# Channel attention and a GELU feed-forward on one core: the second layer of each pair's first chunk by Strassen's scheme over halves, the first layer's products on two PSUM banks

## The chip, the core and the metric

The kernel runs on one core of a Trainium2 chip. The engines that matter here are PE (TensorE: matrix products, each with a load of its stationary operand, a weight load, shown as PEld), DVE (VectorE: elementwise work and sums), ACT (ScalarE: activations and copies) and SP (SyncE, which only issues the DMAs). PE writes its results to PSUM, which has eight banks of 128 x 512 fp32 words; DVE and ACT read them there. The metric is the device time of one execution in microseconds; less is better.

## The reference

```python
def _attn_ref(q, k, v, tau):                      # B, N, C = 4, 6080, 256
    qn = q / (np.linalg.norm(q, axis=1, keepdims=True) + 1e-06)
    kn = k / (np.linalg.norm(k, axis=1, keepdims=True) + 1e-06)
    s = kn.transpose(0, 2, 1) @ qn / tau
    s = s - s.max(-1, keepdims=True)
    a = np.exp(s)
    a /= a.sum(-1, keepdims=True) + 1e-09
    return (v @ a).astype(np.float32)

def _moe_ref(x, w_in, w_out):                     # d_model 256, d_ff 2048
    h = x @ w_in
    g = 0.5 * h * (1.0 + erf(h * inv_sqrt2))
    return (g @ w_out).astype(np.float32)
```

The output is `_moe_ref` of the attention's output, reshaped to 24320 tokens. The attention is over channels, so `a` is only 256 x 256 per batch.

## The kernel before

The 256 x 256 matrix `a` of a batch is folded into the input weights (`w_group`: `e` times `w_in`), so that the rest of a batch is two layers: the hidden values from v (first layer, with a GELU), and the output from the hidden values (second layer, with `w_out`). Every fp32 operand is split into a high part in the reduced fp32 format of PE and a low part that is the difference, and each product is made by three matmuls: high x high, high x low, low x high.

Tokens are in columns. A batch has six *pairs* (`PAIRS`): pair p holds two *chunks* j = 0, 1 of n = 512 tokens each, 480 in the last pair. The hidden dimension of 2048 is cut into eight *units* u of 256, each of two row blocks i = 0, 1. One (b, p, u) is a *step*; there are 4 x 6 x 8 = 192.

- `first_products` makes the four hidden blocks (i, j) of a step by Winograd's form of Strassen's scheme over rows and chunks: seven products in `ORDER`, each of three matmuls of n columns (L459 to L461, tile `ph`), 21 in all. The pool `ps_h` gives it PSUM banks out of four: `one` collects products 0, 2, 4 and 6, `two` products 1 and 5, `three` product 3. ACT copies intermediate sums out (`kept`, L479: p1, p5, u2), DVE adds them to later ones (`added`, L484: h).
- `gelu` (L467 to L469) runs the activation twice on ACT, once into the reduced format (gh) and once in fp32 (g), and DVE subtracts for the low part gl. `plain_products` does the same without Strassen for pair (0,0), before the sums of the weights exist.
- `second_products` multiplies the blocks of the step before with `w_out` (L554 to L556, tile `po`): for each chunk j, row block i and output half c three matmuls, 24 a step. Four banks of `ps_o` collect the eight units of a pair; after the last, ACT and DVE copy them to `osb` (L560, L562) and SP stores them (L567).
- PE alternates: the main loop draws one group of `second_products` after each product of the first layer.

`extras` adds the work that isn't part of the step: `load_wo` (L267, the split `w_out` of a later step, kept in DRAM, three buffers), the loads and splits of v of the next pair (`load_v`, `v_sums`, `v_split` L446, L447), and for the next batch the loads of q and k (L128), their split (`split_qk`, L181 and L182, both on DVE), the score *bursts* (`burst`, L191 and L193, 8 matmuls for each half m, added to `sacc` by DVE, L201), the norms (`norm_part`, L208 load and L209 square on ACT), the softmax in stages, and `w_group`.

The program is written in the order of the loops; a planner then orders each engine's queue by that order and by its own estimate of when an instruction can run, and assigns the buffers of each pool as they come free.

## Time and profile before

| | |
|---|---|
| median of 3 runs | 2198.34 us (2194.01 to 2200.15) |
| profiled execution | 2194.5 us, span of its instructions 2192.7 us |
| busy share of the span | PE 99%, weight loads 82%, DVE 63%, ACT 65% |
| DMA, mean | 122 GB/s, 35.7% of 16 engines |
| weight loads and matmuls | 9664 of each |

A row of a group reads: line, engine, operation, output <- inputs, sizes, count | busy us, mean ns of one | idle time of the engine before them, and what ended it. A row of the timeline reads: start, duration, engine, line, operation, with the idle time before it in brackets. A row of the waits reads: total us, times, longest.

### The profile page before, as it was taken

How to read it: one execution, taken by the hardware profiler on the slowest of the kernel's cores; microseconds unless marked ns; L12 is line 12 of the kernel's file. 1: busy time of each engine (PE TensorE's matmuls, PEld its weight loads, DVE VectorE, ACT ScalarE, POOL GpSimd, SP SyncE). 2: the span in 40 equal slices, each digit the busy share in tenths (PEclk: the TensorE clock that was granted, in tenths of full speed). 3: DMA queues.
4: the chain of work that ended last, by engine and by line, in shares of the span. 5: the costliest groups of instructions: out<-in, count | busy, mean ns of one | idle time of the engine just before them, and what ended most of it. 6: DMA issues, size and time to landing. Idle time of an engine off the chain costs nothing.

```text
span 2192.7 us, 26257 instructions
## 1 busy us (share of the span) xinstructions
PE 2180.0 (99%) x9664; PEld 1792.8 (82%) x9664; DVE 1391.5 (63%) x2186; ACT 1432.3 (65%) x2602; POOL 1.3 (0%) x8
## 2 busy tenths in 40 slices
PE   9999999999999999999999999999999999999999
PEld 7787778888888888888888888888888888888888
DVE  6995757666586675765667657667466555555554
ACT  5678886658866565565766656656576666666665
POOL 0000000000000000000000000000000000000000
PEclk9999999999999999999999999999999999999999
DMA  9467774323752332322224323232122121121121
GB/s 382 171 220 253 243 246 135 105 87 107 254 176 96 97 113 80 121 97 69 97 97 143 119 74 125 78 107 93 49 106 96 58 95 68 68 95 68 68 77 48
DMA packets 77056, 267.52 MB, mean 122 GB/s; under 512 B 7680, under 2 KB 9728, under 8 KB 74880
## 3 DMA queue, kind: packets, MB, share of 16 engines
q1 hardware_dynamic: 76928, 265.84, 35.7%
q8 instruction: 76, 1.25, 0.2%
q14 instruction: 52, 0.43, 0.1%
HBM read 232.52 MB, written 33.29 MB: 121 GB/s over the span
## 4 chain that ended last, share of the span: by engine, by line
PE 89%; ACT 5%; DMA 5%; DVE 1%; issue 0%; SPq 0%; ACTq 0%; DVEq 0%
PE po L556 15%; PE po L554 14%; PE po L555 14%; PE ph L461 12%; PE ph L460 12%; PE ph L459 12%; DMA kqc<-kqt 4%; PE ph L191 3%; ACT kqc L209 2%; PE ph L149 2%; PE ph L531 2%; PE ph L193 1%; ACT gh L467 1%; ACT g L468 1%; PE ph L390 1%; PE ph L388 1%
## 5 line engine op out<-in xcount | busy, mean ns | idle before, releaser
L469 DVE TENSOR_TENSOR gl<-g,gh 128x512 fp32r<-128x512 f32 (+1 forms) x768 | 522.3, 682 | 157.7 <-ACT g L468 155.7
L556 PE MATMUL po<-gh,wo 128*128 128x512 f32 (+1 forms) x1536 | 602.4, 394 | 0.0
L554 PE MATMUL po<-gh,wo 128*128 128x512 f32 (+1 forms) x1536 | 599.0, 390 | 0.0
L555 PE MATMUL po<-gl,wo 128*128 128x512 f32 (+1 forms) x1536 | 596.0, 388 | 1.1 <-DVE gl L469 1.1
L484 DVE TENSOR_TENSOR h<-ph,p 128x512 f32<-128x512 f32 (+1 forms) x368 | 251.6, 684 | 518.8 <-PE ph L461 411.8
L467 ACT ACTIVATE gh<-h 128x512 fp32r<-128x512 f32 (+1 forms) x552 | 345.8, 626 | 283.1 <-DVE h L484 280.8
L459 PE MATMUL ph<-vh,wh 128*128 128x512 f32 (+1 forms) x1288 | 502.8, 391 | 3.0 <-ACT p L479 1.6
L461 PE MATMUL ph<-vh,wl 128*128 128x512 f32 (+1 forms) x1288 | 503.7, 391 | 0.0
L460 PE MATMUL ph<-vl,wh 128*128 128x512 f32 (+1 forms) x1288 | 502.7, 390 | 0.0
L479 ACT COPY p<-ph 128x512 f32<-128x512 f32 (+1 forms) x368 | 213.2, 584 | 245.0 <-PE ph L461 244.7
L555 PEld LDWEIGHTS po<-gl,wo 128*128 128x128 f32 x1536 | 288.3, 188 | 65.6 <-DVE gl L469 2.0
L554 PEld LDWEIGHTS po<-gh,wo 128*128 128x128 f32 x1536 | 288.4, 188 | 62.4 <-ACT wo L246 1.0
L556 PEld LDWEIGHTS po<-gh,wo 128*128 128x128 f32 x1536 | 288.2, 188 | 61.8 <-DVE wo L248 0.5
L468 ACT ACTIVATE g<-h 128x512 f32<-128x512 f32 (+1 forms) x552 | 337.7, 612 | 0.0
L459 PEld LDWEIGHTS ph<-vh,wh 128*128 128x128 f32 x1288 | 242.0, 188 | 58.8 <-ACT p L479 5.0
L460 PEld LDWEIGHTS ph<-vl,wh 128*128 128x128 f32 x1288 | 242.1, 188 | 54.0
L461 PEld LDWEIGHTS ph<-vh,wl 128*128 128x128 f32 x1288 | 241.9, 188 | 49.1
L479 ACT COPY u<-ph 128x512 f32<-128x512 f32 (+1 forms) x184 | 107.1, 582 | 112.9 <-PE ph L461 112.9
L467 ACT ACTIVATE gh<-ph 128x512 fp32r<-128x512 f32 (+1 forms) x216 | 125.1, 580 | 13.0 <-PE po L556 8.3
L484 DVE TENSOR_TENSOR h<-ph,u 128x512 f32<-128x512 f32 (+1 forms) x184 | 125.7, 683 | 3.4
L468 ACT ACTIVATE g<-ph 128x512 f32<-128x512 f32 (+1 forms) x216 | 126.5, 587 | 0.3 <-DVE gl L469 0.3
L191 PE MATMUL ph<-hl 128*128 128x512 f32 x272 | 96.0, 392 | 0.0
(138 smaller groups left out, 1423.2 us busy)
## 6 DMA issues: line engine op xcount, KB each, us to landing
wo<-keep_out SPq DMA_DIRECT2D x184, 512.0 KB, 3.2
raw<-qk SPq DMA_DIRECT2D x95, 512.0 KB, 4.6
kqc<-kqt SPq DMA_DIRECT2D x72, 512.0 KB, 4.5
v_raw<-vt SPq DMA_DIRECT2D x20, 1024.0 KB, 5.0
out<-osb SPq DMA_DIRECT2D x40, 512.0 KB, 3.1
win<-keep_in SPq DMA_DIRECT2D x12, 1024.0 KB, 5.0
raw<-w_in SPq DMA_DIRECT2D x8, 512.0 KB, 7.2
raw<-w_out SPq DMA_DIRECT2D x8, 512.0 KB, 4.4
```

The lines of the kernel that those rows point to most:

```text
L191: nc.tensor.matmul(s, hl[:, 0, j, 0, cs], hl[:, :, j, 1], start=(i == 0), stop=False, skip_group_check=True)
L459: nc.tensor.matmul(ps[:, :n], wh, hi[:, :n], start=start, stop=False, skip_group_check=True)
L460: nc.tensor.matmul(ps[:, :n], wh, lo[:, :n], start=False, stop=False, skip_group_check=True)
L461: nc.tensor.matmul(ps[:, :n], wl, hi[:, :n], start=False, stop=stop, skip_group_check=True)
L467: nc.scalar.activation(out=gh[:, :n], in_=src, func=AF.Gelu)
L468: nc.scalar.activation(out=g[:, :n], in_=src, func=AF.Gelu)
L469: nc.vector.tensor_tensor(out=gl[:, :n], in0=g[:, :n], in1=f32(gh[:, :n]), op=ALU.subtract)
L479: nc.scalar.copy(out=t[:, :n], in_=ps[:, :n])
L484: nc.vector.tensor_tensor(out=h[:, :n], in0=ps[:, :n], in1=t[:, :n], op=ALU.add)
L554: nc.tensor.matmul(o, wo[:, 0, i, cs], gh[:, :n], start=first, stop=False)
L555: nc.tensor.matmul(o, wo[:, 0, i, cs], gl[:, :n], start=False, stop=False)
L556: nc.tensor.matmul(o, wo[:, 1, i, cs], gh[:, :n], start=False, stop=last)
```

## The change

Chunk 1 is computed as before. For chunk 0 the second layer is computed by Winograd's form of Strassen's scheme as well, over the two halves of the chunk's columns, the two row blocks of the unit and the two output halves: seven products of n/2 columns (`work` in `second_products`) in place of four of n. They need sums of the gelu values (`sums`: the activation once in fp32 into `x` by `whole`, three instructions of sums on DVE, the high parts copied by ACT, the low parts subtracted by DVE) and sums of `w_out` (`sum_wo`, made once in pair (0,1), kept in DRAM, loaded for each step by `load_ws`). The seven products go to halves of the banks c00, c01, p0 and p1, which collect over the units; `combine` and `merge` add them up at the end of a pair. It holds for the steps named by `strassen`.

With p0 and p1 in use, the first layer has two banks, h0 and h1 (`ring`, `bank`, `later`), and another `ORDER`. PE's instructions are pinned to the order of the program (`pe`, `mm`). The scores' and weights' high parts are made by ACT instead of DVE (`split_qk`, `w_both`), a step holds one burst or one part of a weight group in place of two, `wo` has two buffers instead of three, the norms' tiles share the ring `raw` (four buffers) and the windows of the input weights the ring `hl` (three).

```diff
-    ps_h = ctx.enter_context(tc.tile_pool(name="ps_h", bufs=4, space=bass.MemoryType.PSUM))
-    ps_o = ctx.enter_context(tc.tile_pool(name="ps_o", bufs=4, space=bass.MemoryType.PSUM))
+    ps = ctx.enter_context(tc.tile_pool(name="ps", bufs=1, space=bass.MemoryType.PSUM))
...
+    def psum(name):
+        return ps.tile([P, NT], F32, name=name)
+
+    ring = deque(("h0", "h1"))
+
     def bank():
-        return ps_h.tile([P, NT], F32, name="ph")
-
+        name = ring.popleft()
+        ring.append(name)
+        return psum(name)
+
+    def later(name):
+        ring.remove(name)
+        ring.append(name)
+
+    def pe(op, *args, **kw):
+        r = op(*args, **kw)
+        if "filled" in state:
+            tc.keep_in_program_order(r)
+        return r
+
+    def mm(*args, **kw):
+        return pe(nc.tensor.matmul, *args, **kw)
...
     def split_qk(b, js):
         raw = raws.pop((b, js))
-        hl = pqk.tile([P, 2, JS, 2, C], F32R, name="hl")
-        nc.vector.tensor_copy(out=hl[:, 0], in_=raw)
+        hl = pqk.tile([P, 2, JS, 2, C], F32R, name="hl", bufs=3)
+        nc.scalar.copy(out=hl[:, 0], in_=raw)
         nc.vector.tensor_tensor(out=hl[:, 1], in0=raw, in1=f32(hl[:, 0]), op=ALU.subtract)
...
     def new_wo(key):
-        wos[key] = pw.tile([P, 2, 2, C], F32R, name="wo", bufs=3)
+        wos[key] = pw.tile([P, 2, 2, C], F32R, name="wo", bufs=2)
...
+    keep_sum = [pdram.tile([P, 2, 4, P], F32, name=f"keep_sum{u}") for u in range(NU)]
+    wss = {}
+
+    def new_ws(key):
+        wss[key] = pw.tile([P, 2, 4, P], F32R, name="ws", bufs=2)
+
+    def load_ws(key):
+        new_ws(key)
+        nc.sync.dma_start(out=f32(wss[key]), in_=keep_sum[key[2]])
+
+    def sum_wo(u):
+
+        wo = wos[0, 1, u]
+        x = pg.tile([P, 2, NT], F32, name="x", bufs=1)
+        full = x[:, 0].rearrange("p (f c) -> p f c", f=2)
+        s1, s2, s3, s4 = (x[:, 1, i * P:(i + 1) * P] for i in range(4))
+        a11, a12, a21, a22 = (full[:, 1 - k, c * P:(c + 1) * P] for c in range(2) for k in range(2))
+        tt = nc.vector.tensor_tensor
+        tt(out=full, in0=f32(wo[:, 0]), in1=f32(wo[:, 1]), op=ALU.add)
+        tt(out=s1, in0=a21, in1=a22, op=ALU.add)
+        tt(out=s3, in0=a11, in1=a21, op=ALU.subtract)
+        tt(out=s2, in0=s1, in1=a11, op=ALU.subtract)
+        tt(out=s4, in0=a12, in1=s2, op=ALU.subtract)
+        new_ws((0, 1, u))
+        ws = wss.pop((0, 1, u))
+        hi, lo = (ws[:, i].rearrange("p s c -> p (s c)") for i in range(2))
+        nc.scalar.copy(out=hi, in_=x[:, 1])
+        tt(out=lo, in0=x[:, 1], in1=f32(hi), op=ALU.subtract)
+        nc.sync.dma_start(out=keep_sum[u], in_=f32(ws))
...
-    def w_group(b, g):
+    def w_part(b, g, m):
...
+        win = wins[b, g]
+        if m == 0:
+            wtmp[g] = pqk.tile([P, 8, 2, P], F32, name="hl", bufs=3)
+        tmp = wtmp[g]
+        cs = slice(m * P, (m + 1) * P)
+        pwt = bank()
+        for d in range(NCT):
+            mm(pwt, eh[:, d, cs], win[:, 0, d], start=(d == 0), stop=False)
+            mm(pwt, eh[:, d, cs], win[:, 1, d], start=False, stop=False)
+            mm(pwt, el[:, d, cs], win[:, 0, d], start=False, stop=(d == NCT - 1))
+        nc.scalar.activation(out=tmp[:, 2 * m:2 * m + 2], in_=pwt.rearrange("p (q r c) -> p r q c", q=2, r=2),
...
+            w_both(whs[g][:, to], wls[g][:, to], tmp[:, of])
...
-    ORDER = ((A11, B11), (S1, T1), (S2, T2), (A12, B21), (S3, T3), (S4, B22), (A22, T4))
+    ORDER = ((A11, B11), (S1, T1), (S2, T2), (S4, B22), (S3, T3), (A12, B21), (A22, T4))
+
+    def passes(o, wh, wl, hi, lo, start, stop):
+        mm(o, wh, hi, start=start, stop=False, skip_group_check=True)
+        mm(o, wh, lo, start=False, stop=False, skip_group_check=True)
+        mm(o, wl, hi, start=False, stop=stop, skip_group_check=True)
...
+    def strassen(b, p, u):
+        return p > 1 if b == 0 else (b, p, u) != (B - 1, NP - 1, NU - 1)
+
+    def gelu(src, n, i, j):
+        if j == 1:
+            gh = pg.tile([P, NT], F32R, name="gh", bufs=2)
+            gl = pg.tile([P, NT], F32R, name="gl", bufs=2)
+        else:
+            gh = pg.tile([P, 4, C] if i == 0 else [P, 3, C], F32R, name=f"gh{i}", bufs=1)
+            gl = pg.tile([P, 4, C] if i == 0 else [P, 3, C], F32R, name=f"gl{i}", bufs=1)
+            gh, gl = (t.rearrange("p k c -> p (k c)") for t in (gh, gl))
...
         return gh, gl
 
+    def whole(src, n, i):
+
+        if i == 1:
+            state["x"] = pg.tile([P, 8 * C], F32, name="x", bufs=1)
+        at = 0 if i == 1 else n
+        nc.scalar.activation(out=state["x"][:, at:at + n], in_=src, func=AF.Gelu)
+
+    def sums(n):
+
+        h = n // 2
+        x = state["x"]
+        b11, b22, b21 = (x[:, k * h:(k + 1) * h] for k in (1, 2, 3))
+        t3, t2, t4 = (x[:, k * h:(k + 1) * h] for k in (5, 6, 7))
+        tt = nc.vector.tensor_tensor
+        hb = pg.tile([P, 3 * C], F32R, name="gh1", bufs=1)
+        lb = pg.tile([P, 3 * C], F32R, name="gl1", bufs=1)
+        ht = pg.tile([P, 4 * C], F32R, name="gh0", bufs=1)
+        lt = pg.tile([P, 4 * C], F32R, name="gl0", bufs=1)
+        state["blocks"]["b"], state["blocks"]["t"] = (hb, lb), (ht, lt)
+        tt(out=x[:, 4 * h:6 * h].rearrange("p (k c) -> p k c", k=2),
+           in0=x[:, h:3 * h].rearrange("p (k c) -> p k c", k=2),
+           in1=x[:, 0:h].unsqueeze(1).broadcast_to([P, 2, h]), op=ALU.subtract)
+        nc.scalar.copy(out=hb[:, :3 * h], in_=x[:, h:4 * h])
+        yield
+        tt(out=t2, in0=t3, in1=b11, op=ALU.add)
+        tt(out=t4, in0=b21, in1=t2, op=ALU.subtract)
+        nc.scalar.copy(out=ht[:, :4 * h], in_=x[:, 4 * h:8 * h])
+        tt(out=lb[:, :3 * h], in0=x[:, h:4 * h], in1=f32(hb[:, :3 * h]), op=ALU.subtract)
+        tt(out=lt[:, :4 * h], in0=x[:, 4 * h:8 * h], in1=f32(ht[:, :4 * h]), op=ALU.subtract)
...
-            t = pg.tile([P, NT], F32, name=name, bufs=2 if name == "p1" else 1)
+            t = pg.tile([P, NT], F32, name=name, bufs=1)
...
+        def chunk0(src, i):
+            if strassen(b, p, u):
+                whole(src, n, i)
+            else:
+                out[i, 0] = gelu(src, n, i, 0)
+
+        name = ring[0]
         one = bank()
         do(0, one, True, False)
         p1 = kept(one, "p1")
@@ -498,18 +593,21 @@
         do(2, one, False, False)
         u2 = kept(one, "u2")
         yield
-        three = bank()
-        do(3, three, True, True)
-        out[1, 0] = gelu(added(three, p1), n)
+        do(3, two, False, True)
+        out[1, 1] = gelu(added(two, u2), n, 1, 1)
         yield
         do(4, one, False, False)
-        out[0, 1] = gelu(added(one, p5), n)
-        yield
-        do(5, two, False, True)
-        out[1, 1] = gelu(added(two, u2), n)
+        out[0, 1] = gelu(added(one, p5), n, 0, 1)
+        yield
+        do(5, two, True, True)
+        chunk0(added(two, p1), 1)
         yield
         do(6, one, False, True)
-        out[0, 0] = gelu(one[:, :n], n)
+        chunk0(one[:, :n], 0)
+        later(name)
+        if strassen(b, p, u):
+            state["sums"] = sums(n)
+            next(state["sums"])
...
     def second_products(b, p, u, blocks):
 
         t0, n = PAIRS[p]
+        h = n // 2
         wo = wos.pop((b, p, u))
-        for j in range(2):
+        mine = strassen(b, p, u)
+        if u == 0:
+            po.clear()
+            po["mixed"] = any(strassen(b, p, x) for x in range(NU))
+            po["plain"] = not all(strassen(b, p, x) for x in range(NU))
+
+        def acc(name):
+            first = name not in po
+            if first:
...
+        def group(i, j, c):
+            o, first = acc(f"c{j}{c}")
+            gh, gl = blocks[i, j]
+            passes(o[:, :n], *wpair(c, i), gh[:, :n], gl[:, :n], first, u == NU - 1 and i == 0)
...
+        for i in (1, 0):
+            for c in range(NCT):
+                group(i, 1, c)
+                if u == NU - 1 and i == 0:
+                    evict(1, c)
+                yield
+        if not mine:
             for i in (1, 0):
-                gh, gl = blocks[i, j]
...
+                    if u == NU - 1 and i == 0:
+                        if po["mixed"]:
+                            merge(b, p, c)
+                            if c == 1:
+                                store(0, po["y"])
                         else:
-                            nc.vector.tensor_copy(out=osb[:, 1, :n], in_=o)
-                            t = b * N + t0 + j * n
-                            dst = out[:, t:t + n].rearrange("(t p) n -> p t n", p=P)
-                            step = 1 if (b, p) == (B - 1, NP - 1) else NCT
-                            for h in range(0, NCT, step):
-                                nc.sync.dma_start(out=dst[:, h:h + step], in_=osb[:, h:h + step, :n])
+                            evict(0, c)
                     yield
+            return
+        ws = wss.pop((b, p, u))
+        (hb, lb), (ht, lt) = blocks["b"], blocks["t"]
+        last = not any(strassen(b, p, x) for x in range(u + 1, NU))
+        work = (("c00", 1, wpair(0, 0), hb, lb, 2), ("p0", 0, wpair(0, 1), hb, lb, 0),
+                ("c00", 0, (ws[:, 0, 3], ws[:, 1, 3]), hb, lb, 1), ("p1", 0, (ws[:, 0, 0], ws[:, 1, 0]), ht, lt, 0),
+                ("p1", 1, (ws[:, 0, 2], ws[:, 1, 2]), ht, lt, 1), ("p0", 1, (ws[:, 0, 1], ws[:, 1, 1]), ht, lt, 2),
+                ("c01", 1, wpair(1, 0), ht, lt, 3))
+        for name, half, w, hi, lo, k in work:
+            o, first = acc(name)
+            passes(o[:, half * h:(half + 1) * h], *w, hi[:, k * h:(k + 1) * h], lo[:, k * h:(k + 1) * h], first, last)
+            if name == "c01":
+                if last:
+                    combine(b, p)
+                    if u == NU - 1:
+                        merge(b, p, 0)
+                        merge(b, p, 1)
+                        store(0, po["y"])
+            yield
...
+    def combine(b, p):
+
+        n = PAIRS[p][1]
+        h = n // 2
+        y = po["y"] = pg.tile([P, NCT, NT], F32, name="osb", bufs=2)
+        p0, p1 = po["p0"], po["p1"]
+        tt = nc.vector.tensor_tensor
+        nc.scalar.copy(out=y[:, 0, h:n], in_=p0[:, 0:h])
+        tt(out=y[:, 0, 0:h], in0=p0[:, h:n], in1=y[:, 0, h:n], op=ALU.add)
+        tt(out=y[:, 1, h:n], in0=p1[:, h:n], in1=y[:, 0, 0:h], op=ALU.add)
+        tt(out=y[:, 1, 0:h], in0=y[:, 1, h:n], in1=p1[:, 0:h], op=ALU.subtract)
+        tt(out=y[:, 0, 0:h], in0=y[:, 0, 0:h], in1=p1[:, 0:h], op=ALU.subtract)
+
+    def merge(b, p, c):
+
+        n = PAIRS[p][1]
+        lo = 0 if c == 0 or po["plain"] else n // 2
+        y = po["y"][:, c, lo:n]
+        nc.vector.tensor_tensor(out=y, in0=po[f"c0{c}"][:, lo:n], in1=y, op=ALU.add)
...
-    pg = ctx.enter_context(tc.tile_pool(name="pg", bufs=5))
+    pg = ctx.enter_context(tc.tile_pool(name="pg", bufs=1))
...
-    with tc.high_priority(), behind("fill"):
-        w_group(0, 0)
     for _ in fill:
         pass
+    ring.extend(("p0", "p1"))
+    with tc.high_priority(), behind("fill"):
+        for m in range(NCT):
+            w_part(0, 0, m)
...
+    def ahead(b, p, u):
+
+        def after(k):
+            i = (b * NP + p) * NU + u + k
+            return i // NU // NP, i // NU % NP, i % NU
+
+        nxt = after(2)
         if nxt[0] < B and nxt[:2] != (0, 0):
             load_wo(nxt)
+        nxt = after(1)
+        if nxt[0] < B and strassen(*nxt):
+            load_ws(nxt)
...
-        if b > 0 and w == 1:
-            w_group(b, NWG - 1)
+        if b > 0 and w == 0:
+            w_part(b, NWG - 1, 1)
...
+            if w in (at, at + 1):
+                burst(b + 1, k, w - at)
+            if w == at + 1:
                 for t in range(NB):
                     hls.pop((b + 1, k * NB + t))
+        for k in range(FILL // NB if b == 0 else 0, NQS // NB):
+            at = start + k * num // den
...
-        if w == 37:
-            state["stages"] = softmax(False, ps_h, "ph")
-        if w >= 37:
+        if w == 36:
+            state["stages"] = softmax(False)
+        if w >= 36:
             next(state["stages"], None)
-        if w in (40, 42, 44, 46):
-            load_win(b + 1, (w - 40) // 2)
-        if w in (42, 44, 46):
-            w_group(b + 1, (w - 42) // 2)
+        if w >= 41:
+            w_part(b + 1, (w - 41) // 2, (w - 41) % 2)
+        if w in (39, 41, 43, 45):
+            load_win(b + 1, (w - 39) // 2)
...
+    second, count = iter(()), 0
...
+        if (b, p) == (0, 1) and u == 0:
+            for name in ("p0", "p1"):
+                ring.remove(name)
         for i, _ in enumerate((plain_products if plain else first_products)(b, p, u)):
-            next(second, None)
+            for _ in range(1 if i < 4 or count < 11 else 2):
+                next(second, None)
...
+        if (b, p) == (0, 1):
+            sum_wo(u)
+        ahead(b, p, u)
         extras(b, p, u)
+        for _ in state.pop("sums", ()):
+            pass
+        count = 11 if strassen(b, p, u) else 8
         second = second_products(b, p, u, state.pop("blocks"))
```

More of the change, by code (lines that the diff above doesn't have):

```diff
@@ L314, in softmax @@
         yield
-        rq = pool.tile([P, NT], F32, name=name)
-        nc.tensor.matmul(rq[:, 0:C], ones, diag.rearrange("p h d -> p (h d)"), start=True, stop=True)
+        rq = psum("c10") if first else bank()
+        mm(rq[:, 0:C], ones, diag.rearrange("p h d -> p (h d)"), start=True, stop=True)
         for m in range(NCT):
@@ L331, in softmax @@
         yield
-        tp = pool.tile([P, NT], F32, name=name)
+        tp = psum("c11") if first else bank()
         tpv = tp.rearrange("p (d c) -> p d c", d=NCT)
```

125 lines of the change are left out of this document (52 added, 73 removed).

## The prediction

> **What bounds the kernel now.** I read the page's head, its 40 slices and its chain first, then TensorE's waits, then the busy time by stretches.
>
> ```profile
> span 2192.7 us, 26257 instructions
> PE 2180.0 (99%) x9664; PEld 1792.8 (82%) x9664; DVE 1391.5 (63%) x2186; ACT 1432.3 (65%) x2602; POOL 1.3 (0%) x8
> PEclk9999999999999999999999999999999999999999
> PE 89%; ACT 5%; DMA 5%; DVE 1%; issue 0%; SPq 0%; ACTq 0%; DVEq 0%
> ...
> PE ph L459 <- ACT p L479: 1.6, 2, 1.2
> PE ph L459 <- ACT u L479: 1.1, 2, 0.8
> PE po L555 <- DVE gl L469: 1.1, 2, 0.6
> ...
> 55.00:165.00 110.00, 108.77 (x467) 85.92 (x466) 106.89 (x211) 77.17 (x148) 0.00 (x0) 1.00 0.58 196
> 165.00:330.00 165.00, 163.16 (x714) 130.49 (x713) 101.41 (x155) 139.97 (x266) 0.00 (x0) 1.00 0.75 246
> 600.00:1100.00 500.00, 499.54 (x2228) 410.34 (x2227) 325.38 (x502) 313.31 (x567) 0.00 (x0) 1.00 0.32 108
> 1600.00:2190.00 590.00, 589.20 (x2602) 487.51 (x2600) 328.71 (x519) 380.76 (x693) 0.00 (x0) 1.00 0.22 77
> ```
>
> TensorE (PE) is busy for 99% of the span at full clock and hardly ever waits for another engine: behind the start, the waits above are its longest, 3.8 us together. The stretches (columns: length, then busy PE, weight load, DVE, ACT, POOL, clock, DMA share, GB/s) say the same of every stage. So time is what PE issues times the pitch of each instruction, and the change must be priced there first. VectorE (DVE) and ScalarE (ACT) come second: 65% busy in the third stretch, but 97% (DVE) in the first and 85% (ACT) in the second.
>
> A matmul's row says 0.39 us, but matmuls overlap; the pitch is the distance between starts:
>
> ```profile
> 1996.17 0.39 PE L461 MATMUL ph<-vh,wl 128*128 128x512 f32 x1
> ...
> 1996.65 0.69 DVE L484 TENSOR_TENSOR h<-ph,p 128x512 f32<-128x512 f32 x1 [4.08 <-PE ph L461]
> ...
> 2000.08 0.39 PE L460 MATMUL ph<-vl,wh 128*128 128x512 f32 x1
> 2000.31 0.39 PE L461 MATMUL ph<-vh,wl 128*128 128x512 f32 x1
> ...
> 2007.02 0.69 DVE L484 TENSOR_TENSOR h<-ph,p 128x512 f32<-128x512 f32 x1 [4.08 <-PE ph L461]
> ...
> 544.03 0.38 PE L461 MATMUL ph<-vh,wl 128*128 128x480 f32 x1
> 544.25 0.38 PE L554 MATMUL po<-gh,wo 128*128 128x480 f32 x1
> 544.47 0.38 PE L555 MATMUL po<-gl,wo 128*128 128x480 f32 x1
> ```
>
> A step (one unit u: 21 first-layer and 24 second-layer matmuls) takes 2007.02 - 1996.65 = 10.37 us, so 10.37/45 = 0.2305 us for 512 columns; 480 columns take 0.2175.
>
> **The change, part by part: the matmuls.** Per step 12 matmuls of chunk 0's second layer (four blocks of three passes) become 7 products x 3 passes = 21 matmuls of half the columns: 256, or 240 in the last pair. All hangs on the pitch of a narrow matmul that loads its own weights. The trace has one neighbour, the score bursts, which alternate 512 and 256 columns, and a floor, 16 matmuls of one column:
>
> ```profile
> 303.54 0.40 PE L191 MATMUL ph<-hl 128*128 128x512 f32 x1
> 303.78 0.28 PE L193 MATMUL ph<-hl 128*128 128x256 f32 x1
> 303.89 0.39 PE L191 MATMUL ph<-hl 128*128 128x512 f32 x1
> ...
> 303.78 0.19 PEld L191 LDWEIGHTS ph<-hl 128*128 128x128 f32 x1
> ...
> 50.30 1.84 PE L172 MATMUL po<-ones,acc 128*128 128x1 f32 x16
> ```
>
> The 256-column matmul starts at 303.78, the next one at 303.89, and the load for that next one also starts at 303.78. So 256 columns hide a whole weight load. Rounded starts give 0.11, half of 0.2305 is 0.115; I take 0.117, the burst's pair (0.35) less a wide one, rounded up. The floor is at most 1.84/16 = 0.115 us for a load with next to no columns: 256 columns lie just above it, and 240, by columns 0.109, may be held by it; I take 0.112 there.
>
> - 512-column step: 12 x 0.2305 - 21 x 0.117 = 2.766 - 2.457 = 0.309 us saved.
> - 480-column step: 12 x 0.2175 - 21 x 0.112 = 2.610 - 2.352 = 0.258 us.
>
> The predicate `strassen` holds in 32 steps of batch 0 (pairs 2 to 5) and in all 144 of batches 1 to 3 but the last: 175, of which 8 + 23 = 31 have n = 480. Saved: 144 x 0.309 + 31 x 0.258 = 44.5 + 8.0 = **52.5 us**. Bounds: with 0.115 and 0.109 it is 60; with 0.132 a matmul it is nothing.
>
> The Trainium skill speaks against this: "TensorE: Matmul & The Clock Gate", Part 3, "The mechanism", says that a weight load overlaps running matmuls only where the row groups differ, and these loads take all 128 rows. By it every one of the 9 added matmuls of a step would show its load. The trace disagrees (load and matmul both start at 303.78, the next matmul 0.11 us later). That rule is rival C below.
>
> **VectorE and ScalarE.** Rows for what is added and removed:
>
> ```profile
> L469 DVE TENSOR_TENSOR gl<-g,gh 128x512 fp32r<-128x512 f32 x640 | 438.7, 688 | 127.5 <-ACT g L468 125.9
> L405 DVE TENSOR_TENSOR wl<-hl,wh 128x1024 fp32r<-128x1024 f32 x12 | 14.7, 1225 | 0.3
> L405 DVE TENSOR_TENSOR wl<-hl,wh 128x768 fp32r<-128x768 f32 x12 | 11.4, 953 | 0.0
> L400 DVE TENSOR_TENSOR hl<-hl 128x256 f32<-128x256 f32 x12 | 5.1, 426 | 13.4 <-ACT hl L391 13.4
> L181 DVE CAST hl<-raw 128x1024 fp32r<-128x1024 f32 x68 | 46.3, 688 | 0.0
> L201 DVE TENSOR_TENSOR sacc<-ph,sacc 128x512 f32<-128x512 f32 x64 | 44.1, 690 | 12.9 <-PE ph L193 12.8
> ...
> L467 ACT ACTIVATE gh<-h 128x512 fp32r<-128x512 f32 x456 | 287.9, 631 | 243.8 <-DVE h L484 243.3
> L468 ACT ACTIVATE g<-ph 128x512 f32<-128x512 f32 x184 | 108.5, 591 | 0.3 <-DVE gl L469 0.3
> L479 ACT COPY p<-ph 128x512 f32<-128x512 f32 x304 | 177.8, 588 | 225.0 <-PE ph L461 225.0
> L350 ACT CAST wh<-hl 128x1024 fp32r<-128x1024 f32 x4 | 4.2, 1047 | 0.0
> ```
>
> DVE a step: removed 2 x 0.69 (gl of chunk 0); added one 512-wide sum 0.69, two 256-wide 0.85, the two low parts 0.95 + 1.22: +2.3 us. ACT: two of four gelus go (-1.2), two copies of 768 (about 0.83, between the 512 and 1024 rows) and 1024 (1.05) come: +0.7. In the third stretch 2228 matmuls of 2400 a batch are 44.6 steps, so a step there has 11.2 us of PE and 7.3 of DVE. After: PE 10.9; DVE 7.3 + 2.3 - 0.45 (the casts of L181 and of the weight parts go to ACT) + 0.27 (`combine`, `merge`) = **9.4 us, 86%**; ACT 7.0 + 0.7 + 0.7 (those casts) = 8.4, 77%, and about 1.26 more where a norm part runs. No engine passes PE, but DVE's reserve shrinks from 35% to 14%.
>
> Does a step stall on its two banks? Lay it out with 0.69 a product and 0.35 a half product (D a first-layer product, S a block of chunk 1 and H a half product of the unit before): D0 S1 D1 S2 D2 S3 D3 S4 D4 H1 H2 D5 H3 H4 D6 H5 H6 H7, 10.06 us. A consumer starts 0.48 us behind the last matmul's start (1996.17 to 1996.65), 0.25 behind the end of its pitch. The sum after D3 (ends 4.84) reads bank `two` until 5.78; D5 needs it at 6.92. The sum after D4 frees `one` at 7.16 for D6 at 8.32; that after D5 frees `two` at 8.56 for the next step at 10.06; the gelu after D6 frees `one` at 9.85 for D1 at 11.44. The copies p5 and u2 leave 1.2 us. The halves are split at about 13.7 and first read at 16.3. So **every bank has 1.1 to 1.6 us of slack: no stall in a plain step**. The cover goes where an extra instruction of that length starts just ahead. This already happens:
>
> ```profile
> 319.27 1.06 ACT L209 ACTIVATE kqc<-kqc 128x1024 f32<-128x1024 f32 x1
> ...
> 320.21 0.20 ACT L209 ACTIVATION_READ_ACCUMULATOR kqc<-kqc 128x1 f32 x1
> 320.30 0.58 ACT L479 COPY p<-ph 128x512 f32<-128x512 f32 x1
> ...
> 320.94 0.50 PE L459 MATMUL ph<-vh,wh 128*128 128x512 f32 x1 [1.23 <-ACT p L479]
> ```
>
> The stalls that I add, each from nothing to its bound:
> - Bursts (68: 64 of L201 and four first copies) take bank `two`; D1 needs it 1.38 us behind the burst. The add is ready at 11.7, DVE ends the 0.95 part at 12.3, adds until 13.0, D1 wanted 12.8: 0.2 each, **14 us**. Half of these steps also hold the 1.22 us subtractions of the split: bound 14 + 34 x 1.22 = 55.
> - Pair ends (23): two steps hold 2 x 7.16 of DVE's own work (three sums 2.07, two gl 1.38, the 3.71 above), seven v subtractions (4.8), a copy, four 256-wide of `combine` and the merges (3.5), bursts and splits (2.5) = 25.1 against 22.0 of PE. That is 3.1 over, but `combine`, `merge` and the last low parts (5 us) may come later, so nothing must stall; bound 23 x 3.1 = 71. I take 0.25 each, **6 us**.
> - Batch ends: 24 weight parts and three softmax tiles now pass through the two banks; their ACT read (0.69) fits D1's 1.2. Bound 24 x 0.7 = 17, I take **3**.
> - Pair (0,1): `sum_wo` adds some 2.6 us of DVE (two of 0.69, four narrow ones of about 0.3) and 0.6 of ACT a step where ACT is at 85% already; splits' casts come on top. Bound 20, I take **4**.
>
> Costed at nothing: PE's pinned order (today's trace alternates D and S in just that order), the shared rings `raw` and `hl`, and `sum_wo`'s stores, which cost only through SP's queue. There `ws` adds 0.5 MB a step (52 GB/s beside 77 to 246), and `wo` in two buffers is loaded one step (10 us) ahead of use instead of two, which still covers its landing of 3.2; an SP wait over 6.8 us ahead of it would cost the rest (today's longest, for the v load, is 10.7).
>
> ```profile
> wo<-keep_out SPq DMA_DIRECT2D x184, 512.0 KB, 3.2
> ...
> SPq L413 <- DVE vl L447: 161.8, 23, 10.7
> ```
>
> Sum: 2194.5 (profiled execution: span 2192.7 plus 1.8 around it) - 52.5 + 27 = 2169. The median of the runs shown is 0.17% above that execution, 2198.3, so 2169 becomes 2173 there; that is my forecast: **2173**.
>
> **The rivals.**
> A, the forecast: stalls give back 10 to 46 us; 2155 to 2192 at the median's scale.
> B, **the bound moves to DVE** (slower). The 128 steps of batch 0 from pair 2 on and of batches 1 and 2 have 9.4 us of DVE in 10.9. If its long instructions, in one fixed order, leave DVE unable to fill more than 82% of the time, a step takes 9.4/0.82 = 11.46, and 128 x 0.56 = 72 us stand in place of the first two terms: 2194.5 - 52.5 + 72 + 7 = 2221, 2225 at the median. It passes the gain where the fill stays under some 83%. For it: two banks in place of four, and the 3.1 us over at pair ends. Against: in the first stretch DVE is 97% full and PE idles for 1.2 us of 110.
> C, the load shows: 21 x (0.117 + 0.112) = 4.81 against 2.77 today, 175 x 2.04 = +357 us: 2552, 2556 at the median. The bursts speak against it; unproven is only a row of narrow matmuls with no wide one between. (It is what the rule of the Trainium skill would do.)
> D, nothing stalls: 2142, 2146 at the median.
> E, stalls of 46 to 59 cancel the gain: within 0.3%.
>
> **How the numbers follow.** A 0.62, D 0.10, E 0.11, B 0.14, C 0.03. A difference under 0.3% can't be told from no change: faster 0.72, same 0.11, slower 0.17. The range takes A, D and E: 2146 to 2205; B and C stay outside.
>
> **What would show it.** In the changed profile: chunk 0's half products start 0.117 us apart in a row (step one); about 11,240 matmuls; DVE some 82% busy over the span; plain steps of 10.06 us in batch 3; PE's waits name the burst's add and the sums of the first layer, some 20 to 30 us, most near bursts and pair ends. Wrong if narrow starts lie 0.13 or more apart, if PE waits for `hb`, `ht` or `ws`, or if steps of batch 1 pass 11.2 us.

## The result, and the profile after

The changed kernel takes **2306.45 us** (median of 4 runs, 2304.96 to 2307.03), the kernel before 2198.82 us beside it (2194.01 to 2200.15). The ratio is 1.0493 with an interval of [1.0474, 1.0511]: 5% slower, where the prediction said 1% faster. That is 101 us above the range.

The head of the page of the changed kernel and its chain come first, in the same form as before:

```profile
span 2305.0 us, 30506 instructions
PE 2188.7 (95%) x11239; PEld 1838.8 (80%) x11239; DVE 1746.6 (76%) x2777; ACT 1639.4 (71%) x2702; POOL 1.3 (0%) x8
...
PE 59%; DVE 14%; ACT 14%; DMA 8%; issue 5%; ACTq 0%; SPq 0%; DVEq 0%
```

PE's idle time is 2305.0 - 2188.7 = 116 us, against 2192.7 - 2180.0 = 13 before. The two shares of DVE and ACT in the chain went from 1% and 5% to 14% each. So the end is set in part by work that PE waits for, although no engine but PE is over 76% busy.

The view of PE's waits (total us, times, longest) says for what:

```profile
PE h L125 <- ACT hl L437: 48.8, 24, 2.4
PE h L125 <- ACT p L567: 24.1, 23, 2.0
PE h L125 <- DVE h L572: 9.1, 16, 1.6
PE h L125 <- DVE sacc L218: 8.3, 14, 1.0
PE p L125 <- DVE hl L265: 4.9, 2, 2.5
PE h L125 <- ACT x L535: 4.8, 5, 1.6
```

Line 437 reads the bank of a weight part (`w_part`), 24 times in all: each one costs 2.0 us. L567 is the copy of an intermediate sum (`kept`), L572 an addition (`added`), L218 the burst's add. All read one of the two banks h0 and h1.

**How the 112 us add up.** In two stages on the page: the span grew by 112.3, of which 103.6 is idle time of PE and 8.7 busy time. By the pitches, busy time should have fallen by 52.5. That it didn't has three reasons. PE's granted clock averaged 0.987 in the changed kernel (1.000 before): at half clock inside some stretches that is 0.013 x 2305/0.5 = 60 us at half speed, which lose 30. And each gap adds 0.27 us of busy time to the pitches: the last row before it lasts 0.40 us in place of 0.23, and the first one behind it starts 0.34 ahead of the next. The 84 waits of the list above turn that into 23 us. With the 512-column pitch (0.2311 us in place of 0.2304, 4 us over some 6,000 matmuls) that makes 57 of the 61.

The saving itself is there. The timeline of the changed kernel in batch 3, and the stretch of its pairs 0 to 4 (length, then busy PE, weight load, DVE, ACT, POOL, clock, DMA share, GB/s):

```profile
2015.40 0.69 DVE L572 TENSOR_TENSOR h<-h,u 128x512 f32<-128x512 f32 x1 [0.64 <-PE h L125]
...
2018.15 0.28 PE L125 MATMUL c<-gh,ws 128*128 128x256 f32 x1
2018.27 0.28 PE L125 MATMUL p<-gh,ws 128*128 128x256 f32 x1
2018.38 0.28 PE L125 MATMUL p<-gl,ws 128*128 128x256 f32 x1
...
2022.54 1.05 ACT L556 CAST gh<-x 128x1024 fp32r<-128x1024 f32 x1 [0.67 <-DVE x L555]
...
2025.49 0.69 DVE L572 TENSOR_TENSOR h<-h,u 128x512 f32<-128x512 f32 x1 [0.64 <-PE h L125]
```

```profile
600.00:1100.00 500.00, 478.17 (x2495) 401.02 (x2496) 384.06 (x590) 367.17 (x597) 0.00 (x0) 0.99 0.48 164
...
1830.00:2200.00 370.00, 370.00 (x1979) 317.52 (x1978) 285.67 (x442) 273.50 (x444) 0.00 (x0) 1.00 0.35 128
```

Half products start 0.117 us apart, a plain step takes 2025.49 - 2015.40 = 10.09 us (10.06 was forecast, 10.37 before), and in 370 us of batch 3 PE isn't idle once. In the third stretch of before, a batch now has 2400 + 48 x 9 = 2832 matmuls, so 2495 of them are 42.3 steps: 11.8 us a step, against 11.2 before and 10.9 forecast.

**One of the 24 stalls in full.** The timeline of the changed kernel, batch 0, last pair; PE has just made a weight part into bank h and wants the bank for a product of the first layer:

```profile
569.78 0.80 ACT L552 CAST gh<-x 128x720 fp32r<-128x720 f32 x1
...
570.07 0.39 PE L125 MATMUL h<-hl,el 128*128 128x512 f32 x1
...
570.80 0.90 DVE L557 TENSOR_TENSOR gl<-x,gh 128x720 fp32r<-128x720 f32 x1
...
571.62 0.40 DVE L555 TENSOR_TENSOR x<-x 128x240 f32<-128x240 f32 x1
572.11 0.99 ACT L556 CAST gh<-x 128x960 fp32r<-128x960 f32 x1 [1.53 <-DVE x L555]
573.01 0.68 ACT L437 ACTIVATE hl<-h,rden 128x512 f32<-128x512 f32 x1
...
573.74 0.56 PE L125 MATMUL h<-vh,wh 128*128 128x480 f32 x1 [1.98 <-ACT hl L437]
574.10 0.60 PE L125 MATMUL h<-vl,wh 128*128 128x480 f32 x1
...
574.50 0.60 PE L125 MATMUL h<-vh,wl 128*128 128x480 f32 x1
```

Read it backward. PE waits for the read L437. By 570.55 its data were there (the last matmul of the part starts at 570.07 and a consumer starts 0.48 behind). But L437 stands on ACT's queue behind L556, the copy of `ht`, and L556 waits for `t4` (L555), which DVE runs behind L557, the low part `lb` of 0.90 us. ACT does nothing for 1.53 us while ready work stands behind the instruction that waits. In the program L555 is written before L557; the planner put `lb` first. In a plain step of pairs 0 to 4 `lb` stands ahead of `t4` as well, but it is harmless there: the copy p1 (L567) comes before L556 on ACT, L556 waits for 0.67 us only (the row at 2022.54 above), and the copy p5 behind it is still in time. In the last pair of batch 3 p1 stands behind L556, and L567 takes the place of L437 six times:

```profile
2224.60 0.99 ACT L556 CAST gh<-x 128x960 fp32r<-128x960 f32 x1 [1.53 <-DVE x L555]
2225.50 1.01 ACT L567 COPY p<-h 128x480 f32<-128x480 f32 x2
2226.11 0.49 PE L125 MATMUL h<-vh,wh 128*128 128x480 f32 x1 [1.96 <-ACT p L567]
```

The last three rows of the stall in batch 0 show the second loss: the same 480-column matmuls now start 0.36 to 0.40 us apart, not 0.217. The stretch up to the end of this stall, and the one behind it, show the clock:

```profile
569.00:573.70 4.70, 2.76 (x13) 1.97 (x11) 2.77 (x5) 3.14 (x6) 0.00 (x0) 1.00 0.66 227
573.70:577.20 3.50, 3.46 (x9) 2.91 (x10) 3.16 (x6) 2.68 (x4) 0.00 (x0) 0.54 0.00 0
```

A gap of 2.0 us is followed by 3.41 us at clock 0.5, in which PE does 9 matmuls, not 16. The records have 16 stretches at half clock in the changed kernel, 60 us in all: 14 of 3.41 us, one of 10.2 us near 72 to 82, and one of 2.4 us at the very end, where the kernel before has its only one, of 0.9 us.

### The profile page after: what moved, and what is told of

The parts are those of the page before. It is cut to its first block, busy times and chain, and to the rows that moved or that the text cites. A ratio compares the mean times of both kernels' runs of the same rounds, so it can differ in the third digit from the quotient of the medians.

```text
span 2305.0 us, 30506 instructions
## 1 busy us (share of the span) xinstructions
PE 2188.7 (95%) x11239; PEld 1838.8 (80%) x11239; DVE 1746.6 (76%) x2777; ACT 1639.4 (71%) x2702; POOL 1.3 (0%) x8
## 4 chain that ended last, share of the span: by engine, by line
PE 59%; DVE 14%; ACT 14%; DMA 8%; issue 5%; ACTq 0%; SPq 0%; DVEq 0%
PE h L125 29%; PE c L125 21%; PE p L125 7%; DMA raw<-kqt 7%; DVE h L572 3%; ACT x L535 3%; ACT raw L226 2%; DVE gl L557 2%; ACT gh L525 2%; PE h L167 2%; ACT gh L556 2%; DVE hl L200 2%; ACT g L526 2%; DVE x L549 2%; DVE gl L558 1%
## 5 line engine op out<-in xcount | busy, mean ns | idle before, releaser
L125 PE MATMUL c<-gh,wo 128*128 128x512 f32 (+3 forms) x2372 | 840.0, 362 | 0.0
L125 PE MATMUL h<-vh,wh 128*128 128x512 f32 (+1 forms) x1312 | 533.8, 407 | 99.6 <-ACT hl L437 48.8
L125 PE MATMUL h<-vl,wh 128*128 128x512 f32 (+1 forms) x1312 | 519.3, 396 | 0.0
L125 PE MATMUL h<-vh,wl 128*128 128x512 f32 (+1 forms) x1312 | 518.7, 395 | 0.0
L125 PEld LDWEIGHTS c<-gh,wo 128*128 128x128 f32 x2372 | 451.6, 190 | 76.2
L525 ACT ACTIVATE gh<-h 128x512 fp32r<-128x512 f32 (+1 forms) x402 | 250.4, 623 | 265.3 <-DVE h L572 246.9
L125 PE MATMUL c<-gl,wo 128*128 128x512 f32 (+3 forms) x1186 | 425.4, 359 | 0.0
L125 PEld LDWEIGHTS h<-vh,wh 128*128 128x128 f32 x1312 | 249.7, 190 | 183.1 <-ACT hl L437 58.5
L572 DVE TENSOR_TENSOR h<-h,p 128x512 f32<-128x512 f32 (+1 forms) x368 | 249.9, 681 | 64.5 <-PE h L125 56.0
L125 PEld LDWEIGHTS h<-vh,wl 128*128 128x128 f32 x1312 | 249.8, 190 | 53.7
L125 PEld LDWEIGHTS h<-vl,wh 128*128 128x128 f32 x1312 | 250.1, 191 | 31.0 <-DVE vl L495 0.3
L567 ACT COPY p<-h 128x512 f32<-128x512 f32 (+1 forms) x368 | 211.4, 580 | 80.8 <-PE h L125 80.5
L556 ACT CAST gh<-x 128x1024 fp32r<-128x1024 f32 (+1 forms) x175 | 181.8, 1039 | 78.2 <-DVE x L555 77.2
L572 DVE TENSOR_TENSOR h<-h,u 128x512 f32<-128x512 f32 (+1 forms) x184 | 125.6, 683 | 110.5 <-PE h L125 109.2
```

Of the source, the lines that this page charges most:

```text
L125: r = op(*args, **kw)
L525: nc.scalar.activation(out=gh[:, :n], in_=src, func=AF.Gelu)
L556: nc.scalar.copy(out=ht[:, :4 * h], in_=x[:, 4 * h:8 * h])
L567: nc.scalar.copy(out=t[:, :n], in_=ps[:, :n])
L572: nc.vector.tensor_tensor(out=h[:, :n], in0=ps[:, :n], in1=t[:, :n], op=ALU.add)
```

## The experiments

Two theories stood against each other. **Queues (Q):** the loss is the order of work on ACT's and DVE's in-order queues, where a read that would free a bank stands behind an instruction that waits. **Banks and DVE (the rival, B):** two banks are too few, or DVE has too much to do, whatever the order (rival B of the prediction). Each kernel was timed beside the kernel before on the same chip. Gains below are taken between the differences of this table.

| run | us (median) | before beside it | difference | ratio [interval] |
|---|---|---|---|---|
| the change | 2306.45 | 2198.82 | +107.6 | 1.0493 [1.0474, 1.0511] |
| e1_two_banks | 2230.43 | 2196.26 | +34.2 | 1.0164 [1.0149, 1.0179] |
| e2_no_sums | 2232.40 | 2196.26 | +36.1 | 1.0168 [1.0153, 1.0183] |
| e3_lb_behind | 2253.48 | 2196.26 | +57.2 | 1.0269 [1.0253, 1.0284] |
| e3_both | 2228.47 | 2196.26 | +32.2 | 1.0159 [1.0142, 1.0176] |
| e4_vsums | 2219.91 | 2197.40 | +22.5 | 1.0100 [1.0078, 1.0121] |
| e4_wcopy | 2230.73 | 2197.40 | +33.3 | 1.0160 [1.0137, 1.0183] |
| e4_unpin | 2220.30 | 2197.40 | +22.9 | 1.0110 [1.0091, 1.0130] |
| e4_all | 2214.77 | 2197.40 | +17.4 | 1.0081 [1.0061, 1.0101] |
| e5_light | 2190.88 | 2195.76 | -4.9 | 0.9980 [0.9971, 0.9989] |
| e5_four_banks | 2219.57 | 2195.76 | +23.8 | 1.0111 [1.0097, 1.0125] |
| e5_batch3 | 2196.02 | 2195.76 | +0.3 | 1.0000 [0.9991, 1.0009] |
| e6_batch3_free | 2182.55 | 2195.39 | -12.8 | 0.9943 [0.9930, 0.9957] |

**e1_two_banks: the rest of the change without Strassen's scheme in the second layer.**

```diff
     def strassen(b, p, u):
-        return p > 1 if b == 0 else (b, p, u) != (B - 1, NP - 1, NU - 1)
+        return False
...
-            gh = pg.tile([P, 4, C] if i == 0 else [P, 3, C], F32R, name=f"gh{i}", bufs=1)
+            gh = pg.tile([P, NT], F32R, name=f"gh{i}", bufs=2)
...
-        if (b, p) == (0, 1):
-            sum_wo(u)
...
```

> The second layer of chunk 0 as before (four blocks of three full-width passes, no sums of the gelus, no sums of w_out), everything else of the change kept: two banks for the first layer, PE's pinned order, high parts of the scores and weights on ACT. Theory Q (ACT's queue: the copy of the second part of the sums stands ahead of the read that frees a PSUM bank): without the sums there is nothing to stand ahead, so about the time before plus the bursts' waits, 2200 to 2225 us, and the reads of the weight parts (L437 in the changed kernel) no longer hold PE for 2 us each. Theory B (two banks are too few whatever stands in the queues): most of the loss stays, 2270 us or more (the whole 158 us of added waits without the 52 us of gain would give 2350).

It took 2230.43 us, just above the range of the queue theory and far from the rival's. What the change does around the scheme costs 34 us by itself; its longest group of waits (view of PE's waits) is small and scattered:

```profile
PE h L125 <- ACT g L525: 10.0, 20, 1.9
```

L525 is the gelu that frees a bank. The scheme saves 52.5 us of pitch and yet adds 108 - 34 = 74, so it brings about 126 us of loss with it.

**e2_no_sums: half products without the sums.** The seven products take the halves of plain gelu blocks.

```diff
-            if strassen(b, p, u):
-                whole(src, n, i)
-            else:
-                out[i, 0] = gelu(src, n, i, 0)
+            out[i, 0] = gelu(src, n, i, 0)
...
-            state["sums"] = sums(n)
-            next(state["sums"])
...
-        (hb, lb), (ht, lt) = blocks["b"], blocks["t"]
+        (hb, lb), (ht, lt) = blocks[1, 0], blocks[0, 0]
...
```

> Leaves out the sums of the gelu values: the 21 half-width matmuls of chunk 0 read halves of the plain gelu blocks, split as before (two activations and one subtraction a block). PE's instructions are those of the changed kernel. Theory Q: PE gets its shorter work without the chain x, sums, copy, so 2150 to 2185 us. Theory B (two banks) or a dearer pitch of the half products: 2240 us or more.

2232.40 us lies between the two and decides less than hoped, in part because the edit brought a wait of its own: without `whole`, two activations hold the bank in place of one. PE's waits in this run:

```profile
PE h L125 <- ACT g L525: 20.6, 38, 1.3
```

The waits at L437 are off the list, though: with the sums gone, so are they. Still, it takes as long as e1, which has the wide products: PE is busy for 30 us less than in e1 (2166.6 against 2197.0) and idle for 30 us more (64.4 against 34.7). So the shorter steps bring waits even without the sums, which the range of the queue theory left out.

**e3_lb_behind and e3_both: nothing left out, only the order.** The first keeps `lb` behind `t4` on DVE. The second also keeps ACT's copy of `ht` behind the copy p1 of the next step, so that nothing that waits for `t4` stands ahead of a read that frees a bank.

```diff
-        tt(out=t4, in0=b21, in1=t2, op=ALU.subtract)
-        nc.scalar.copy(out=ht[:, :4 * h], in_=x[:, 4 * h:8 * h])
-        tt(out=lb[:, :3 * h], in0=x[:, h:4 * h], in1=f32(hb[:, :3 * h]), op=ALU.subtract)
+        done = tt(out=t4, in0=b21, in1=t2, op=ALU.subtract)
+        with tc.issue_after(done.ins):
+            tt(out=lb[:, :3 * h], in0=x[:, h:4 * h], in1=f32(hb[:, :3 * h]), op=ALU.subtract)
+        yield
+        with tc.issue_after(state["p1"].ins):
+            nc.scalar.copy(out=ht[:, :4 * h], in_=x[:, 4 * h:8 * h])
...
```

> One order on DVE alone: the subtraction for the low part of the first three blocks (0.95 us) is put behind the last sum t4 instead of ahead of it, so that ACT's copy of the second part can start about 0.95 us earlier. Theory Q: the 30 stalls of about 2.2 us (24 at weight parts, 6 in the last pair) shrink by 0.95 each, some 28 us, and some of the half-clock stretches behind them go (13 of them, 1.7 us each): 2260 to 2280 us. Theory B: within 5 us of 2306.

> Two orders: that on DVE, and on ACT the copy of the second part of the sums goes behind the copy p1 of the next step, so that it stands ahead of no read that frees a bank before p1. Theory Q: the 30 stalls (65 us) and the half-clock stretches behind them (13 x 1.7 = 22 us) go: about 2306 - 87 = 2219 us, 2205 to 2235. Theory B: 2290 us or more, the waits move to other reads of the two banks.

The first took 2253.48 us, below what was expected (50 us less than the change), the second 2228.47, inside its range (75 us less). PE's waits in the first, then in the second:

```profile
PE h L125 <- ACT hl L437: 32.8, 24, 1.7
PE h L125 <- ACT p L568: 14.2, 19, 1.4
```

```profile
PE h L125 <- ACT p L570: 19.4, 17, 3.7
PE h L125 <- DVE h L575: 11.1, 13, 2.7
```

With `lb` behind, each wait at L437 is shorter by about 0.7 us of the 0.90 that `lb` takes; with both edges the group is off the list, and the same place in the timeline of e3_both reads:

```profile
574.43 0.68 ACT L437 ACTIVATE hl<-h,rden 128x512 f32<-128x512 f32 x1
575.07 0.56 ACT L570 COPY p<-h 128x480 f32<-128x480 f32 x1
575.52 1.00 ACT L560 CAST gh<-x 128x960 fp32r<-128x960 f32 x1
```

The read, then the copy, then `ht`: two edges in the order, with all work kept, take back 75 of the 108 us. That shows the queue theory for the largest part. The first edge gained more than expected, and the clock came back with it: at waits of up to 1.7 us at L437, none of the 14 stretches of 3.41 us is left, and 11.9 us at half clock remain of 60 (mean clock 0.998), which is worth about 24 of the 50 us. In e3_both it is 34.8 us (mean clock 0.992): its waits are fewer, but some are longer (up to 3.7 us at L570).

**e4: what is left of it, one edit each on top of e3_both.** e4_vsums keeps `v_sums` of the next pair behind the step's h, e4_wcopy gives the copies of the weights' high parts back to DVE, e4_unpin pins PE's order from pair (0,1) on and not from the start, and e4_all has all three.

```diff
+                    if "h" in state:
+                        stack.enter_context(tc.issue_after(state["h"].ins))
                     v_sums(*pair, u - 4)
...
-            w_both(whs[g][:, to], wls[g][:, to], tmp[:, of])
+            nc.vector.tensor_copy(out=whs[g][:, to], in_=tmp[:, of])
+            tt(out=wls[g][:, to], in0=tmp[:, of], in1=f32(whs[g][:, to]), op=ALU.subtract)
...
-        if "filled" in state:
+        if "pinned" in state:
             tc.keep_in_program_order(r)
...
```

The first was tried because of this place in the timeline of e3_both, where DVE waits for a DMA ahead of the addition that PE needs:

```profile
625.40 0.69 DVE L476 TENSOR_TENSOR vs<-v_raw 128x512 f32<-128x512 f32 x1 [1.62 <-DMA v_raw<-vt]
...
631.21 0.50 PE L125 MATMUL h<-vh,wh 128*128 128x512 f32 x1 [2.69 <-DVE h L575]
```

> On top of both orders (2228 us): the four sums over v of the next pair are kept behind the last first-layer sum h of the step in which the program has them; the planner had put them on DVE's queue a pair end earlier, ahead of an h that PE waits for, where they also wait for the DMA of v. Theory Q (a queue's head holds a read that frees a bank): the stalls of 2.9, 2.9 and 2.2 us at the first step of a batch go and with them a half-clock stretch or two: 2212 to 2222 us. Rival B (the two banks lack slack, whatever waits): the waits move, within 4 us of 2228.

> On top of both orders: the high parts of the weights of batches 1 to 3 are copied by DVE as before the change, not by ACT. Theory Q: the copy on ACT waits for DVE's sums and holds p1 of the next step behind it (3.7, 2.5 and 3.9 us at the second step of a batch); without it 10 us and some half-clock time go: 2212 to 2222 us. Rival: DVE is the scarce engine there, so the 1.25 us a group that it gets back cost as much: 2225 us or more.

> On top of both orders: PE's instructions are pinned to the program's order only behind pair (0,0). Theory P (the pinned order makes PE wait at the start for weight windows that DVE hasn't narrowed yet): 8 us of waits at 71 to 78 us and the half-clock stretch of 10 us behind them (5 us) go: 2212 to 2220 us. Rival: the order makes no difference there, DVE is full in that pair: within 3 us of 2228.

> Both orders and the three edits together. Theory Q with P: 2228 less about 10, 12 and 13 us: 2188 to 2200 us, level with the kernel before or 0.5% faster. Rival B: 2215 us or more.

e4_vsums gained 10 us, inside its range, and e4_unpin 9, at the edge of its own. e4_wcopy gained nothing (2230.73): its rival held. The waits only changed their engine, as PE's waits of that run show beside e3_both's L570 and L575 above:

```profile
PE h L125 <- DVE h L576: 29.1, 20, 4.2
PE h L125 <- ACT p L571: 3.6, 5, 1.0
```

And e4_all, at 2214.77, gained 15 and missed its range; it lies at the edge of the rival's. The stretch at the start of batch 1 and the timeline there show what is left:

```profile
600.00:645.00 45.00, 38.11 (x191) 32.13 (x190) 39.48 (x64) 30.19 (x51) 0.00 (x0) 0.92 0.43 151
```

```profile
632.20 0.39 PE L125 MATMUL h<-vh,wl 128*128 128x512 f32 x1
...
634.17 1.22 DVE L200 TENSOR_TENSOR hl<-raw,hl 128x1024 fp32r<-128x1024 f32 x1
635.30 0.69 DVE L454 CAST wh<-hl 128x1024 fp32r<-128x1024 f32 x1
635.90 1.22 DVE L562 TENSOR_TENSOR gl<-x,gh 128x1024 fp32r<-128x1024 f32 x1
637.04 1.22 DVE L455 TENSOR_TENSOR wl<-hl,wh 128x1024 fp32r<-128x1024 f32 x1
638.17 0.69 DVE L576 TENSOR_TENSOR h<-h,u 128x512 f32<-128x512 f32 x1
```

DVE is busy for 39.48 of 45 us. The addition that frees the bank (L576) had its data from about 632.68 on (the last matmul of its product starts at 632.20, and a consumer starts 0.48 behind), but it ran at 638.17: seven other instructions stood ahead of it on DVE, the last four of which are shown. So this is a place in a queue again, now in a queue with little room. An edge that puts this addition first wasn't run, so order and load aren't told apart here.

**e5_light: how much of the rest hangs on DVE.** e4_all without the subtractions `lb` and `lt`; the matmuls read the high parts in place of the low ones.

```diff
-        tt(out=lt[:, :4 * h], in0=x[:, 4 * h:8 * h], in1=f32(ht[:, :4 * h]), op=ALU.subtract)
...
-        state["blocks"]["b"], state["blocks"]["t"] = (hb, lb), (ht, lt)
+        state["blocks"]["b"], state["blocks"]["t"] = (hb, hb), (ht, ht)
...
```

> On top of the four edits of the kernel of 2215 us: leaves out the two subtractions that make the low parts of the seven blocks (0.95 and 1.22 us of DVE a step; the matmuls read the high parts a second time), PE's instructions, banks and orders as they are. Theory D (what is left of the loss is DVE without room: at bursts and pair ends its queue holds a row of 0.7 to 1.2 us instructions ahead of the h or the burst's add that frees a bank): of the 65 us of waits above those before the change most go, 2155 to 2185 us. Rival B (two banks lack slack by themselves): 2200 us or more.

2190.88 us lies between the ranges of the theory and the rival; against the kernel before it is 22 us better than e4_all. By PE's waits, first of e4_all, then of this kernel, DVE's part fell from 32.3 to 6.7 us, and ACT's came up:

```profile
PE h L125 <- DVE h L576: 22.9, 17, 4.2
PE h L125 <- DVE sacc L218: 9.4, 15, 1.4
```

```profile
PE h L125 <- ACT p L566: 20.1, 16, 1.9
PE h L125 <- DVE h L571: 6.7, 8, 1.4
```

So the two subtractions are worth about 22 us at this point, by their time and their places in the queue together, and some 20 us of waits at ACT's copies stay. In the trace each of these 16 copies stands on ACT's queue behind the square of a norm part (L226, 1.06 us, 10 times, 11.3 us of waits) or the exponential of the softmax with a table load of 1.28 us (L374, 6 times, 8.8 us); no run took those away.

**e5_four_banks: e1 with four banks for the first layer.** It keeps p0 and p1 in the ring.

```diff
-        if (b, p) == (0, 1) and u == 0:
-            for name in ("p0", "p1"):
-                ring.remove(name)
```

> The kernel without Strassen in the second layer and without its sums (2230 us with two banks), now with four banks for the first layer throughout. Theory: of its 34 us over the time before, the start (pinned order in pair (0,0), about 13 us with its half-clock stretch) stays and the waits for the two activations on one bank (15 us) go: 2208 to 2218 us. Rival (two banks cost nothing here, the rest of the rearrangement does): 2225 us or more.

2219.57 us, between the two expectations and near the first: two banks cost 10 of e1's 34 us, and the other 24 come from the rest of the rearrangement. The start is 9 of them, if it costs here what e4_unpin gained.

**e5_batch3 and e6_batch3_free: the scheme only where nothing stands beside it.** Batch 3 has no bursts, splits or weight parts for a next batch, and from 1830 to 2200 us it had no stall (those of its last pair come from the order that the two edges mend). Both kernels have the edits of e4_all, and use Strassen's scheme in the second layer, and two banks, in the 47 steps of batch 3 alone (elsewhere chunk 0's blocks of the odd units lie in the tile x, so that the memory suffices). The first pins PE's order from pair (0,1) on, the second from batch 3 on.

```diff
     def strassen(b, p, u):
-        return p > 1 if b == 0 else (b, p, u) != (B - 1, NP - 1, NU - 1)
+        return b == B - 1 and (b, p, u) != (B - 1, NP - 1, NU - 1)
...
-        if (b, p) == (0, 1) and u == 0:
-            state["pinned"] = True
         if (b, p) == (B - 1, 0) and u == 0:
+            state["pinned"] = True
             for name in ("p0", "p1"):
                 ring.remove(name)
...
```

(The first pair of lines is in both; the part behind the dots is the step from e5_batch3 to e6_batch3_free.)

> The four edits, with Strassen in the second layer and two banks in the last batch alone (47 steps), where no bursts, norms or weight parts run beside it; four banks and the old second layer before. If a plain step is worth 0.309 us (0.26 in the last pair): 39 x 0.309 + 8 x 0.26 = 14 us less than the kernel before, 2183 us, at most 8 us more for what the rearrangement costs elsewhere (2183 to 2191). If two banks or the sums cost something in plain steps too: 2197 us or more.

> The kernel with the changed second layer in the last batch alone (2196 us), its PE order pinned from that batch on instead of from pair (0,1). Theory P: the 11 us of waits that it has above the kernel before stand where PE may not pass a matmul that waits (the softmax at the end of a batch, 2.3 us each, and the first steps of a batch, 1.0 us each); left free, the planner fills them as before and the 14 us of the 47 steps come out: 2183 to 2190 us. Rival: the waits stand on ACT's and DVE's queues, which are the same, so PE finds nothing to put there: within 3 us of 2196.

The first took 2196.02 us, as long as before, and missed its range. Its timeline in a softmax tile shows one of the waits:

```profile
521.95 1.28 ACT L374 ACT_TABLE_LOAD   x1
...
523.75 1.00 ACT L575 COPY p<-p 128x480 f32<-128x480 f32 x2
524.34 0.49 PE L125 MATMUL p<-vh,wh 128*128 128x480 f32 x1 [2.13 <-ACT p L575]
```

A table load of 1.28 us on ACT, with the exponential behind it, makes a copy late; PE, pinned to the order of the program, stands still for 2.13 us. Without the pin in batches 0 to 2 the second took **2182.55 us** (2182.38 to 2184.34; ratio 0.9943, [0.9930, 0.9957]), 12.8 us less than before and 0.5 us below its range: 0.6% faster than the kernel before. The head of its page:

```profile
span 2181.1 us, 27424 instructions
PE 2168.1 (99%) x10087; PEld 1800.0 (83%) x10087; DVE 1478.1 (68%) x2337; ACT 1538.1 (71%) x2684; POOL 1.3 (0%) x8
```

PE is back at 99% of its span, as before the change, with 423 matmuls more. 40 steps x 0.309 + 7 x 0.258 = 14.2 us were to be had there by the prediction's own terms, and 12.8 came.

## Why the prediction was wrong

- **The matmuls (52.5 us saved): right.** Between two 256-column matmuls the starts are 117 ns apart (median of 2599), 112 for 240 columns, 11,239 matmuls in all, and batch 3 alone gives most of its share (12.8 of 14.2 us). The subtraction that the text gives for 0.117 doesn't yield it, though (0.35 less 0.2305 is 0.1195, which would have saved 45 us); the bursts of the trace before have 0.117 as the median of 273 such starts. Rival C, the visible weight load, is out. By the rule of the Trainium skill, "TensorE: Matmul & The Clock Gate", Part 3, "The mechanism", each of these full-row loads would have shown; the row of half products above, 0.117 us apart, disagrees.
- **The layout of a plain step (10.06 us, no stall): right** for pairs 0 to 4 of batch 3 (10.09, PE never idle in 370 us). In the last pair of batch 3, where nothing stands beside the steps either, six of them stalled for 1.8 to 2.0 us each. It was used for batches 0 to 2 as well, where it isn't the plain step that stalls.
- **Bursts 14 and the first layer's additions at pair ends 6: right in kind and near in size.** The waits at L218 are 8.3 us, those at L572 9.1, of which about 5.5 at pair ends.
- **"Batch ends: 24 weight parts ... I take 3" failed, and it is the step that decides.** The text set the length of ACT's read (0.69) against the slack of 1.2 and bounded the term by 24 x 0.7 = 17. It measured 48.8, nearly three times the bound, since the read was not late by its own length but by what stood ahead of it on ACT's queue: a copy that waited for DVE, which did a 0.90 us subtraction first. No line of the working asked what the planner puts ahead of that read. The layout took `t4` before `lb`, the order of the program, not the planner's. e3_both shows this cause: two edges, 75 us.
- **No term for the norm parts.** The text shows a copy held up behind one (L209) and then lists no stall for it. In the changed kernel 12 of the 23 waits at L567 stand behind one, 8.9 us.
- **"Costed at nothing: PE's pinned order" failed.** It costs 9 us at the start of the program (e4_unpin) and 13 us over batches 0 to 2 beside the softmax and the batch starts (e5_batch3 against e6_batch3_free, with four banks and the old second layer there). The trace before alternates products in the same order, but there the planner was free to put other work ahead of a product that it expected late.
- **The clock was no term at all.** Some 30 us of the loss are matmuls at half clock behind the stalls, so a stall of 2 us cost up to 3.41/2 = 1.7 us more than itself.
- **Rival B, the slower one, had the sign and a part of the cause.** DVE isn't the bound of the kernel (76% over the span, under the 82% at which the rival put the fill), but once the order is mended, leaving out two of its subtractions is worth about 22 us, at bursts and batch starts (e5_light). The chance given to B, 0.14, went to the right sign with a price of 2225; most of the loss was the term above.
- **What would show it wrong** was named in part: steps of batch 1 pass 11.2 us (11.8). PE's waits come to 110 us where 20 to 30 were expected, and the longest group, the read of the weight parts, wasn't among those named.

What stays open: whether another order would take back the waits that e4_all has on DVE's queue and e5_light on ACT's, and the split of the 15 us of e1 that neither the banks nor the start explain. Moving `ht` alone, without `lb`, wasn't tried, and the 4 us for pair (0,1) weren't measured apart.

## What to carry to other kernels

When a change takes buffers away, the price is not the length of the read that frees one but the place of that read in its engine's queue: list for each such read what the engine runs just ahead of it, and what that waits for. A layout by plain steps prices plain steps; the stalls sit where something rare (a weight part, a softmax tile, a batch's start) meets the new order, so price those from the queues that the planner makes, not from the order of the program. And a saving that is real but needs slack can be applied to the stage that has it, as batch 3 here.
